# One store of a head's attention outputs in place of four, and a shorter probabilities' ring with the value products further behind, in a fused adaLN + cached attention + mixer MLP kernel

## The chip, the cores and the metric

The kernel runs on one core of one Trainium2 chip. A core has a matrix engine (TensorE, PE in the profile; its weight loads are shown as PEld), a vector engine (VectorE, DVE), a scalar engine (ScalarE, ACT), a general engine (GpSimd, POOL) and a sync engine (SP), which here only issues DMA transfers. Each takes its instructions in order, and they meet at semaphores. PSUM is the memory that matmuls write to, SBUF the working memory; DMA transfers run beside the engines.

The metric is the device time in microseconds (us) of one execution, as the median of several runs.

## The reference

One sequence of 2048 tokens of width 640, 32 attention heads of 128 with cached keys and values (2048 of each), and a mixer MLP; everything is bf16. Cut to what matters:

```python
mod = (silu(c) @ w_mod).reshape(1, 6, 1, -1)            # sa, ca, ga, sb, cb, gb
h = layernorm(x) * (1 + ca) + sa
q = (h @ wq), in heads                                  # 32 x 2048 x 128
p = softmax(q k^T * 128 ** -0.5)                        # per head 2048 x 2048
x = x + ga * ((p v), heads side by side) @ wo
h = layernorm(x) * (1 + cb) + sb
g = gelu(layernorm(h) @ w1); four column groups shifted by +1, -1, +2, -2 rows
x1 = h + shifted(g) @ w2
x = x + gb * (x1 + gelu(layernorm(x1) @ w3) @ w4)
```

## The kernel before, in words

Every operation is put in the program through a small helper, `Prog`, with the keys that it reads and writes; the helper works out the semaphore waits from them. The order on each engine is the order in which the program's loops write the operations down. There is no planner.

**Attention.** The work is cut in 512 tiles: 32 heads of 16 query tiles of 128 rows. A loop over steps s (line 506) writes down for each step what belongs to different tiles:

- the scores of tile s, in two halves of 1024 keys (`qk`, line 286, TensorE), into the PSUM tile `Sps`;
- the value product of tile s - `PVD`, `PVD` = 8 (`pv`, line 299, TensorE), also in two halves, in between the halves of the scores. Its weights are the transposed probabilities `PTs`; the values carry a column of ones, so that the row sums come with it;
- a part of the next head's query projection (`q_piece`, line 237);
- for every second finished product a copy from PSUM to `Of` (line 537, ScalarE);
- VectorE reduces each half of the scores to a minimum and writes the negated, scaled scores to `negS`, which has three slots (line 546). GpSimd takes the minimum of the two halves (line 556). ScalarE makes the exponential from `negS` with this bias (line 559), into `Pb`, a ring of `RP` = 10 slots, one tile each;
- the probabilities are transposed from `Pb` into `PTs`, a second ring of `RP` slots. Tiles 3 and 10 of a head are transposed on TensorE (`t_piece`, line 253) and evicted by ScalarE (line 262), one of the four halves by VectorE (line 264). The other fourteen go through DMA transposes that SP issues (`transpose`, line 222), two neighbours in one transfer where both are there: six pairs and two single tiles for a head;
- SP also issues the loads of the next heads' keys (line 205, step 2 of a head), query weights (line 209, step 6) and values (line 214, step `PVD` + 1 = 9). All of SP's transfers stand in one queue, in the order of the loop;
- `LAG` = 4 steps after its product GpSimd normalises a tile (`norm`, line 447) with the inverse row sums (`rcp`, line 440, for four tiles) into `On`, which has two buffers of four tiles. After each fourth tile GpSimd issues a store of 128 KB to `o_scratch` in DRAM (line 454), laid out [8, 128, 32, 2, 128]: pair of query tiles, row, head, tile of the pair, column. A piece that lies together there is 512 bytes, the two tiles of one row and head.

A product thus needs its probabilities transposed `PVD` steps after its scores; an exponential needs the slot of `Pb` of the tile `RP` before it read; a transpose needs the slot of `PTs` of the tile `RP` before it multiplied.

**After attention.** `load_ot` (line 495, SP) reads a pair of query tiles of all heads back from `o_scratch` with a transpose; then follow the output projection (line 618, TensorE), layer norms (lines 599 to 644) and the MLP (lines 706 to 769). These stages reuse SBUF: the rings hold `xt`, `xb` and one of the two buffers `gT` of the MLP's hidden activations, `On` holds statistics, `wo` holds `w3`, `w4` and the output's staging.

Of the kernel before, what the change touches and what calls it, by code (L numbers as in the profile page):

```python
# [7 lines left out]
BF16 = mybir.dt.bfloat16  # L8
# [107 lines left out]
def bass_adaLN_cond__mha_block_cached__mixer_s_mlp__prompt_kernel(  # L116
# [21 lines left out]
    with ExitStack() as es:  # L138
# [11 lines left out]
        if True:  # L150
            with ExitStack() as es1:
                sb1 = lambda name, shape, dt: es1.enter_context(nc.sbuf_tensor(name, shape, dt))
                RP = 10
                PVD = 8
# [3 lines left out]
                ring = sb1("ring", [128, 2 * RP, SK], BF16)  # L158
# [6 lines left out]
                On = sb1("On", [128, 2, 4, 128], BF16)  # L165
# [12 lines left out]
                Pb = ring[:, 0:RP]  # L178
                PTs = ring[:, RP:2 * RP].rearrange("p r (k q) -> p r k q", k=NKT)
# [5 lines left out]
                RO = 13 * SK  # L185
# [11 lines left out]
                assert CO + 8 * KT <= 2 * RP * SK and XO + NQT * D <= WO_ and WO_ + KT * 2 * D <= 10 * SK  # L197
# [19 lines left out]
                assert RP % 2 == 0 and NQT % 2 == 0  # L217
                is_pe = lambda g: g % NQT in PE_TILES

                def transpose(g, n):  # L220
                    b = g % RP
                    G.dma("sync", lambda e: e.dma_start_transpose(
                        PTs[:, b:b + n].rearrange("p r k q -> p (r k) q"), ring[:, b:b + n].rearrange("p r s -> p (r s)")),
                        ("t", b), r=[("Pb", b + i) for i in range(n)], w=[("PT", b + i, z) for i in range(n) for z in range(2)])
# [22 lines left out]
                def t_piece(g, r, q):  # L247
                    jb = bank(("t", g, r))

                    def f(t):  # L250
                        for z in range(4 * q, 4 * q + 4):
                            kt = 8 * r + z
                            ins = t.transpose(JBb[jb][:, z * 128:(z + 1) * 128], Pb[:, g % RP, kt * 128:(kt + 1) * 128], ident[:])
                        return ins
                    G.op("tensor", f, r=[("Pb", g % RP)], w=[("J", jb)])

                def t_evac(g, r):
                    jb = bank(("t", g, r))
                    dst = PTs[:, g % RP, r * 8:(r + 1) * 8, :]
                    src = JBb[jb].rearrange("p (k q) -> p k q", k=8)  # L260
                    if not by_dve(g, r):
                        G.op("scalar", lambda a: a.copy(dst, src), r=[("J", jb)], w=[("PT", g % RP, r)])  # L262
                    else:
                        G.op("vector", lambda v: v.tensor_copy(dst, src), r=[("J", jb)], w=[("PT", g % RP, r)])
# [27 lines left out]
                def pv(g, half):  # L292
                    hb = (g // NQT) % 2
                    b = g % RP
                    ob = PO[:, ((g // 2) % 2) * 512 + (g % 2) * 130:]

                    def f(t):
                        for kt in range(half * 8, half * 8 + 8):
                            ins = t.matmul(ob[:, 0:129], PTs[:, b, kt, :], Vaug[:, hb, kt, 0:129],  # L299
                                           start=(kt == 0), stop=(kt == NKT - 1))  # L300
# [3 lines left out]
                ringk = lambda a, b: [k for i in range(a // SK, -(-b // SK)) for k in (  # L304
                    [("Pb", i)] if i < RP else [("PT", i - RP, 0), ("PT", i - RP, 1)])]
                WMK = ringk(WO_, WO_ + KT * 2 * D)
                WRK = ringk(RO, 2 * RP * SK)
# [137 lines left out]
                def norm(gr, z):  # L445
                    b = gr % 2
                    G.op("gpsimd", lambda g: g.tensor_scalar(  # L447
                        out=On[:, b, z, :], in0=Of[:, 2 * b + z // 2, z % 2, 0:128],
                        scalar1=rl[:, 4 * b + z:4 * b + z + 1], scalar2=1.0, op0=ALU.mult, op1=ALU.mult),
                        r=[("Of", 2 * b + z // 2), ("rl", b)], w=[("On", b, z)])  # L450
                    if z < 3:
                        return
                    hh, jj = divmod(4 * gr, NQT)
                    G.dma("gpsimd", lambda e: e.dma_start(  # L454
                        o_scr[jj // 2:jj // 2 + 2, :, hh].rearrange("a p z d -> p a (z d)"),
                        On[:, b].rearrange("p (a z) d -> p a (z d)", a=2)),
                        ("o", b), r=[("On", b, z) for z in range(4)], w=[("os", b), ("osd", jj // 4, hh)])
# [5 lines left out]
                assert GT0 + NFT4 <= 2 * RP * SK  # L463
# [4 lines left out]
                gT = [flat[:, GT0:GT0 + NFT4].rearrange("p (f q) -> p f q", f=NFT),  # L468
                      negb[:, 0:NFT4].rearrange("p (f q) -> p f q", f=NFT)]
# [11 lines left out]
                sm = On[:].rearrange("p a z d -> p (a z d)").bitcast(F32)  # L481
# [4 lines left out]
                mhalf = sm[:, 384:385]  # L486
                NEG = [("negS", i) for i in range(3)]
# [3 lines left out]
                ONK = [("On", b, z) for b in range(2) for z in range(4)]  # L491
# [14 lines left out]
                for s in range(NG + PVD + LAG):  # L506
                    h, j = divmod(s, NQT)
                    g_ = s - PVD
# [26 lines left out]
                    if 0 <= g_ < NG and g_ % 2 == 1:  # L535
                        p = g_ // 2
# [18 lines left out]
                    if s < NG:  # L555
# [4 lines left out]
                            Pb[:, s % RP, :], negS[:, s % 3, :], ACT.Exp, bias=nm[:, r8:r8 + 1], scale=-1.0),  # L560
                            r=[("negS", s % 3), ("nm", r8)], w=[("Pb", s % RP)])
# [11 lines left out]
                    if 0 <= s - PVD - LAG:  # L573
                        gr, z = divmod(s - PVD - LAG, 4)
# [3 lines left out]
                    if s == NG:  # L578
# [3 lines left out]
                    if s == NG + 1:  # L582
# [154 lines left out]
                def d_op(cc, f_):  # L737
# [9 lines left out]
                    G.op("scalar", lambda a: a.activation(gT[g][0:fsz[f_], f_, :], JB[jb][0:fsz[f_], :], GELU),  # L747
                         r=[("J", jb)], w=[("gT", g)] + ([("OT", 1)] if g == 1 and f_ == 0 else []))

                def e_op(j):  # L750
# [5 lines left out]
                    def f(t):  # L756
                        for c0, cw in NC2:
                            for f_ in range(NFT):
                                ins = t.matmul(YB[b][:, c0:c0 + cw], gT[g][0:fsz[f_], f_, q0:q0 + 128], w4[0:fsz[f_], f_, c0:c0 + cw],  # L759
# [71 lines left out]
```

## Time and profile before

| what | value |
|---|---|
| median of three runs | 1615.55 us (1611.88 to 1622.05) |
| span of the profiled execution, first to last instruction | 1613.0 us, 34611 instructions |
| granted TensorE clock, mean | 0.993 |
| busy: PE, DVE, ACT, POOL | 92%, 86%, 80%, 39% of the span |
| DMA | 333.60 MB, mean 207 GB/s |
| last exponential of attention ends | about 1264 us |

No time of the profiled execution beyond its span is recorded; the median of the runs is 2.5 us above the span.

How to read the lines that follow: a group's row gives the line, the engine, the operation and the tiles written and read, then the number of instructions, their busy time and the mean of one in ns, and behind the last bar the idle time of the engine just before them with what ended it. A row of the waits gives the waiting engine and line, what ended the wait, the total in us, how often, and the longest. A row of the timeline gives the start in us, the duration, the engine (SPq is SP's queue) and the line; "x5" means that five neighbouring instructions are merged in the row; in square brackets stands the idle time before it. A queue's row gives its packets, megabytes and the time that its packets took, as a share of 16 engines' span.

### The profile page before, as it was taken

Reading aid. Unit: us, or ns where it says so; the run is one execution under the profiler, and the core shown is the slowest. Engines: PE = TensorE matmul, PEld = TensorE weight load, DVE = VectorE, ACT = ScalarE, POOL = GpSimd, SP = SyncE. Lnnn points to the kernel's source line nnn. Section 1 sums busy time; section 2 is a strip of 40 time slices with the busy share of each in tenths; the row PEclk is TensorE's granted clock in tenths of the full one; section 3 lists DMA queues with packets and bytes.
Section 4 is the critical chain, followed back from the end, with each engine's and each line's share of the span. In section 5 each row is a group of like instructions: output and inputs, shape, how many; then the busy total and the mean of one; then the engine's idle time right before and its main releaser. Section 6 shows DMA issues by size and latency. Waiting matters only on the chain.

```text
span 1613.0 us, 34611 instructions
## 1 busy us (share of the span) xinstructions
PE 1489.2 (92%) x13978; PEld 962.9 (60%) x14231; DVE 1394.3 (86%) x2460; ACT 1294.9 (80%) x1145; POOL 622.8 (39%) x1394
## 2 busy tenths in 40 slices
PE   5899999999999999999999999999999799999998
PEld 3466666666666666666666666666666555545444
DVE  6999999999999999999999999999999256665424
ACT  4999999999999999999999999999999300055330
POOL 0244444444444444444444444444444323222000
PEclk9999999999999999999999999999999799999999
DMA  9999999999999999999999999999999995530000
GB/s 305 231 230 234 243 238 235 241 242 242 233 243 236 244 232 242 238 235 238 242 249 229 245 237 233 245 237 233 241 237 245 214 213 105 105 111 1 17 17 34
DMA packets 1167728, 333.60 MB, mean 207 GB/s; under 512 B 1148304, under 2 KB 1161552, under 8 KB 1167568
## 3 DMA queue, kind: packets, MB, share of 16 engines
q1 hardware_dynamic: 1161424, 314.59, 97.5%
q0 software_dynamic: 6144, 16.79, 3.4%
q8 instruction: 112, 1.84, 0.5%
q14 instruction: 48, 0.39, 0.1%
HBM read 43.48 MB, written 19.40 MB: 39 GB/s over the span
## 4 chain that ended last, share of the span: by engine, by line
ACT 29%; DVE 24%; PE 21%; DMA 16%; issue 8%; POOL 2%; SPq 0%; POOLq 0%; DVEq 0%
ACT ring L559 23%; DVE negS L546 22%; DMA ring<-ring 13%; PE Sps L618 7%; PE Sps L759 4%; ACT ring L262 2%; PE Oaug L743 2%; PE QPp L743 2%; ACT Of L537 1%; ACT kv L244 1%; PE Sps L728 1%; PE PTp L299 1%; DMA ring<-in_A_x_dram 1%; POOL small L556 1%; PE Sps L286 1%
## 5 line engine op out<-in xcount | busy, mean ns | idle before, releaser
L546 DVE TENSOR_SCALAR_CACHE_REDUCE negS<-Sps 128x1024 f32<-128x1024 f32 x1024 | 1179.0, 1220 | 30.3 <-PE Sps L286 29.5
L559 ACT ACTIVATE ring<-negS,small 128x2048 bf16<-128x2048 f32 x512 | 1029.3, 2017 | 22.7 <-POOL small L556 20.5
L299 PEld LDWEIGHTS PTp<-kv,ring 128*128 128x128 bf16 x8192 | 553.0, 98 | 313.0 <-DMA ring<-ring 97.4
L299 PE MATMUL PTp<-kv,ring 128*128 128x129 bf16 x8192 | 647.9, 221 | 51.2 <-DMA ring<-ring 49.1
L286 PE MATMUL Sps<-kv 128*128 128x512 bf16 x1950 | 592.3, 381 | 35.6 <-DVE negS L546 18.1
L556 POOL TENSOR_SCALAR small<-small 128x1 f32<-128x1 f32 x512 | 145.9, 285 | 631.2 <-DVE negS L546 631.2
L286 PEld LDWEIGHTS Sps<-kv 128*128 128x128 bf16 x2048 | 144.7, 97 | 139.6 <-DVE negS L546 94.6
L447 POOL TENSOR_SCALAR On<-Of,small 128x128 bf16<-128x128 f32 x512 | 189.9, 371 | 13.4 <-DMA o_scratch<-On 0.5
L656 ACT COPY kv<-PTp 128x640 bf16<-128x640 bf16 x32 | 22.0, 692 | 154.8 <-PE PTp L653 154.8
L440 POOL TENSOR_TENSOR small<-Of,small 128x4 f32<-128x4 f32 x128 | 133.1, 1040 | 6.7 <-ACT Of L537 6.7
L454 POOL DMA_DIRECT2D o_scratch<-On x128 | 103.1, 806 | 40.8 <-POOL On L447 37.2
L537 ACT COPY Of<-PTp 128x259 f32<-128x259 f32 x256 | 95.7, 374 | 11.1 <-PE PTp L299 11.1
L237 PE MATMUL Oaug<-hTx,kv 128*128 128x512 bf16 x264 | 100.4, 385 | 3.9 <-DVE hTx L396 3.9
L237 PE MATMUL QPp<-hTx,kv 128*128 128x512 bf16 x259 | 97.7, 382 | 2.7 <-ACT hTx L391 2.2
L546 DVE DVE_READ_ACCUMULATOR negS<-Sps 128x1 f32 x1024 | 85.8, 84 | 0.0
L599 POOL TENSOR_SCALAR On<-On 128x1 f32<-128x1 f32 x48 | 24.3, 507 | 152.2 <-DVE On L608 152.2
L626 DVE TENSOR_TENSOR ring<-Sps,mod_bc 128x640 f32<-128x640 f32 x16 | 13.2, 824 | 77.6 <-PE Sps L618 77.6
L618 PE MATMUL Sps<-wo,hTx 128*128 128x128 bf16 (+1 forms) x504 | 71.2, 303 | 5.3 <-DMA hTx<-o_scratch 4.9
L618 PE MATMUL Sps<-wo,negS 128*128 128x128 bf16 (+1 forms) x504 | 69.1, 298 | 1.5 <-DMA negS<-o_scratch 1.1
L763 DVE TENSOR_TENSOR ring<-Sps,ring 128x640 f32<-128x640 f32 x16 | 13.2, 824 | 66.2 <-PE Sps L759 66.2
L262 ACT COPY ring<-Oaug 128x1024 bf16<-128x1024 bf16 x64 | 65.2, 1019 | 0.0
L618 PEld LDWEIGHTS Sps<-wo,hTx 128*128 128x128 bf16 x512 | 40.2, 99 | 36.6 <-DMA hTx<-o_scratch 4.8
(82 smaller groups left out, 1004.2 us busy)
## 6 DMA issues: line engine op xcount, KB each, us to landing
kv<-in_A_v_cache_dram SPq DMA_DIRECT2D x32, 512.0 KB, 5.0
o_scratch<-On POOLq DMA_DIRECT2D x128, 128.0 KB, 3.8
ring<-in_A_x_dram SPq DMA_DIRECT2D x8, 640.0 KB, 5.1
kv<-in_A_wq_dram SPq DMA_DIRECT2D x32, 160.0 KB, 3.4
wo<-in_A_wo_dram SPq DMA_DIRECT2D x1, 5120.0 KB, 16.5
ring<-ring SPq DMA_TRANSPOSE x256, 7.0
ring<-in_w_mod_dram SPq DMA_DIRECT2D x1, 3200.0 KB, 13.5
out_dram<-wo SPq DMA_DIRECT2D x16, 160.0 KB, 1.8
```

Of the source, the lines that this page charges most:

```text
L237: G.op("tensor", lambda t: t.matmul(JB[jb], wq[:, hb, q, :], hT[:, q, cc * 512:(cc + 1) * 512], start=(q == 0), stop=(q == KT - 1)), r=[(" ...
L262: G.op("scalar", lambda a: a.copy(dst, src), r=[("J", jb)], w=[("PT", g % RP, r)])
L286: ins = t.matmul(Sps[:, col:col + 512], QT[:, hb, j * 128:(j + 1) * 128], KTs[:, hb, col:col + 512], start=True, stop=True)
L299: ins = t.matmul(ob[:, 0:129], PTs[:, b, kt, :], Vaug[:, hb, kt, 0:129], start=(kt == 0), stop=(kt == NKT - 1))
L440: G.op("gpsimd", lambda g: g.tensor_tensor(out=rl[:, 4 * b:4 * b + 4], in0=Of[:].rearrange("p a z d -> p (a z) d")[:, 4 * b:4 * b + 4, 128 ...
L447: G.op("gpsimd", lambda g: g.tensor_scalar(out=On[:, b, z, :], in0=Of[:, 2 * b + z // 2, z % 2, 0:128], scalar1=rl[:, 4 * b + z:4 * b + z ...
L454: G.dma("gpsimd", lambda e: e.dma_start(o_scr[jj // 2:jj // 2 + 2, :, hh].rearrange("a p z d -> p a (z d)"), On[:, b].rearrange("p (a z) d ...
L537: G.op("scalar", lambda a, p=p: a.copy(Of[:, p % 4].rearrange("p z d -> p (z d)")[:, 0:259], PO[:, (p % 2) * 512:(p % 2) * 512 + 259]), r= ...
L546: G.op("vector", lambda v, half=half, s=s, r8=r8: v.tensor_scalar(out=negS[:, s % 3, half * 1024:(half + 1) * 1024], in0=Sps[:, half * 102 ...
L556: G.op("gpsimd", lambda g, r8=r8: g.tensor_scalar(out=nm[:, r8:r8 + 1], in0=nm0[:, r8:r8 + 1], scalar1=nm1[:, r8:r8 + 1], scalar2=None, op ...
L559: G.op("scalar", lambda a, s=s, r8=r8: a.activation(Pb[:, s % RP, :], negS[:, s % 3, :], ACT.Exp, bias=nm[:, r8:r8 + 1], scale=-1.0), r=[( ...
L618: ins = t.matmul(YB[b][:, c0:c0 + cw], OTj[pr % 2][:, 2 * hh + z, :], wo[:, hh, c0:c0 + cw], start=(hh == 0), stop=(hh == H - 1))
```

## The change

The ring of probabilities `Pb` gets 8 slots (`RPB`), the ring of transposed ones keeps 10 (`RPT`). The value products run 10 steps behind the scores (`PVD`); near the end of the last head the distance shrinks to 8 (`PVE`), by a table `PVS` of which products belong to which step, so that the last ones come in the same step as before. The values' load, at step `PVD` + 1 of a head, moves from step 9 to 11. `On` holds two whole heads, and a head's sixteen normalised tiles are stored by one transfer of 512 KB after its last tile; the last head still stores four tiles at a time. Tiles that shared the freed memory move: `wmodr` in the set-up, and in the MLP the first buffer `gT`, which is now in three pieces (in the ring, in `On`, and in the rest of `wo`).

```diff
-                RP = 10
-                PVD = 8
+                RPB, RPT = 8, 10
+                PVD, PVE = 10, 8
...
-                ring = sb1("ring", [128, 2 * RP, SK], BF16)
+                ring = sb1("ring", [128, RPB + RPT, SK], BF16)
...
-                On = sb1("On", [128, 2, 4, 128], BF16)
+                On = sb1("On", [128, 2, NQT, 128], BF16)
...
-                RO = 13 * SK
+                RO = 10 * SK
...
                 def transpose(g, n):
-                    b = g % RP
+                    b, t = g % RPB, g % RPT
                     G.dma("sync", lambda e: e.dma_start_transpose(
-                        PTs[:, b:b + n].rearrange("p r k q -> p (r k) q"), ring[:, b:b + n].rearrange("p r s -> p (r s)")),
-                        ("t", b), r=[("Pb", b + i) for i in range(n)], w=[("PT", b + i, z) for i in range(n) for z in range(2)])
+                        PTs[:, t:t + n].rearrange("p r k q -> p (r k) q"), ring[:, b:b + n].rearrange("p r s -> p (r s)")),
+                        ("t", b), r=[("Pb", b + i) for i in range(n)], w=[("PT", t + i, z) for i in range(n) for z in range(2)])
...
                 def norm(gr, z):
                     b = gr % 2
+                    hh, jj = divmod(4 * gr + z, NQT)
                     G.op("gpsimd", lambda g: g.tensor_scalar(
-                        out=On[:, b, z, :], in0=Of[:, 2 * b + z // 2, z % 2, 0:128],
+                        out=On[:, hh % 2, jj, :], in0=Of[:, 2 * b + z // 2, z % 2, 0:128],
                         scalar1=rl[:, 4 * b + z:4 * b + z + 1], scalar2=1.0, op0=ALU.mult, op1=ALU.mult),
-                        r=[("Of", 2 * b + z // 2), ("rl", b)], w=[("On", b, z)])
-                    if z < 3:
+                        r=[("Of", 2 * b + z // 2), ("rl", b)], w=[("On", hh % 2, jj)])
+                    n = 4 if hh == H - 1 else NQT
+                    if jj % n < n - 1:
                         return
-                    hh, jj = divmod(4 * gr, NQT)
+                    j0 = jj + 1 - n
                     G.dma("gpsimd", lambda e: e.dma_start(
-                        o_scr[jj // 2:jj // 2 + 2, :, hh].rearrange("a p z d -> p a (z d)"),
-                        On[:, b].rearrange("p (a z) d -> p a (z d)", a=2)),
-                        ("o", b), r=[("On", b, z) for z in range(4)], w=[("os", b), ("osd", jj // 4, hh)])
+                        o_scr[j0 // 2:(j0 + n) // 2, :, hh].rearrange("a p z d -> p a (z d)"),
+                        On[:, hh % 2, j0:j0 + n, :].rearrange("p (a z) d -> p a (z d)", z=2)),
+                        ("o", hh % 2, j0 if n < NQT else 0), r=[("On", hh % 2, j0 + i) for i in range(n)],
+                        w=[("osd", i, hh) for i in range(j0 // 4, (j0 + n) // 4)])
...
+                def gT(g, f_):
+                    if g == 1:
+                        return negb[:, f_ * 512:f_ * 512 + 512]
+                    if f_ < g0:
+                        return flat[:, GT0 + f_ * 512:GT0 + f_ * 512 + 512]
+                    if f_ < g0 + g1:
+                        return Onf[:, 1024 + (f_ - g0) * 512:1024 + (f_ - g0) * 512 + 512]
+                    return gx[:, (f_ - g0 - g1) * 512:(f_ - g0 - g1) * 512 + 512]
...
                 LAG = 4
-                for s in range(NG + PVD + LAG):
+                PVS, at = {}, []
+                for g in range(NG):
+                    d = max(PVE, min(PVD, PVE + (NG - 12 - g) // 2))
+                    at.append(max(g + d, at[-1] if g else 0))
+                    PVS.setdefault(at[g], []).append(g)
+                assert all(len(v) <= 2 for v in PVS.values())
+                NORMS = {}
+                for g in range(NG):
+                    NORMS.setdefault(at[g] + LAG, []).append(g)
+                OT0 = max(NG, at[NG - NQT + 3] + LAG + 1)
+                for s in range(at[-1] + LAG + 1):
                     h, j = divmod(s, NQT)
-                    g_ = s - PVD
+                    pvs = PVS.get(s, [])
...
-                        if 0 <= g_ < NG:
-                            pv(g_, half)
+                        for g_ in pvs:
+                            if len(pvs) == 1:
+                                pv(g_, half)
+                            elif g_ == pvs[half]:
+                                pv(g_, 0)
+                                pv(g_, 1)
...
                         G.op("scalar", lambda a, s=s, r8=r8: a.activation(
-                            Pb[:, s % RP, :], negS[:, s % 3, :], ACT.Exp, bias=nm[:, r8:r8 + 1], scale=-1.0),
-                            r=[("negS", s % 3), ("nm", r8)], w=[("Pb", s % RP)])
+                            Pb[:, s % RPB, :], negS[:, s % 3, :], ACT.Exp, bias=nm[:, r8:r8 + 1], scale=-1.0),
+                            r=[("negS", s % 3), ("nm", r8)], w=[("Pb", s % RPB)])
...
-                    if 0 <= s - PVD - LAG:
-                        gr, z = divmod(s - PVD - LAG, 4)
+                    for g_ in NORMS.get(s, []):
+                        gr, z = divmod(g_, 4)
                         if z == 0:
                             rcp(gr)
                         norm(gr, z)
-                    if s == NG:
+                    if s == OT0:
                         load_ot(0)
```

For the 512 tiles of this case `OT0` is step 512, as before.

More of the change, by code (lines that the diff above doesn't have):

```diff
@@ L177, in bass_adaLN_cond__mha_block_cached__mixer_s_mlp__prompt_kernel @@
                 QT = kv[:, o3:o3 + 2 * SQ].rearrange("p (b q) -> p b q", b=2)
-                Pb = ring[:, 0:RP]
-                PTs = ring[:, RP:2 * RP].rearrange("p r (k q) -> p r k q", k=NKT)
+                Pb = ring[:, 0:RPB]
+                PTs = ring[:, RPB:RPB + RPT].rearrange("p r (k q) -> p r k q", k=NKT)
                 flat = ring[:].rearrange("p r s -> p (r s)")
@@ L293, in pv @@
                     hb = (g // NQT) % 2
-                    b = g % RP
+                    b = g % RPT
                     ob = PO[:, ((g // 2) % 2) * 512 + (g % 2) * 130:]
@@ L490, in bass_adaLN_cond__mha_block_cached__mixer_s_mlp__prompt_kernel @@
                 HTK = [("hT", cc, k) for cc in range(NQC) for k in range(KT)]
-                ONK = [("On", b, z) for b in range(2) for z in range(4)]
+                ONK = [("On", b, z) for b in range(2) for z in range(NQT)]
                 OFK = [("Of", b) for b in range(4)]
@@ L534, in bass_adaLN_cond__mha_block_cached__mixer_s_mlp__prompt_kernel @@
                                     evacs.append((t_evac, g, r))
-                    if 0 <= g_ < NG and g_ % 2 == 1:
-                        p = g_ // 2
+                    for p in [g_ // 2 for g_ in pvs if g_ % 2 == 1]:
                         G.op("scalar", lambda a, p=p: a.copy(
```

35 lines of the change are left out of this document (19 added, 16 removed).

## The prediction

> **What bounds the kernel now.** I began with the groups by cost and the queues of the page, went on to the list of waits, and then to the timeline of SP's queue, which decides.
>
> ```profile
> q1 hardware_dynamic: 1161424, 314.59, 97.5%
> q0 software_dynamic: 6144, 16.79, 3.4%
> ...
> L546 DVE TENSOR_SCALAR_CACHE_REDUCE negS<-Sps 128x1024 f32<-128x1024 f32 x1024 | 1179.0, 1220 | 30.3 <-PE Sps L286 29.5
> ...
> PEld PTp L299 <- DMA ring<-ring: 97.4, 105, 3.1
> ```
>
> The attention stage runs to about 1264 us, and in it VectorE is nearly full. Two of its 1024-wide reductions start 1.144 us apart in the timeline, so a head needs 16 x 2.288 + 0.60 (its one eviction of line 264) = 37.2 us. It idles 30.3 us in all, for late scores; by heads, 6.0 of that lies in the first. TensorE stands in order behind value products (line 299) that wait for DMA transposes, and its scores come late for that. So at most 24 us can be won from such waits. ScalarE is no refuge: by the distance of starts (1.90 us an exponential, 0.25 an `Of` copy, 0.46 a `QT` copy, 0.89 an eviction of line 262) a head costs it 30.4 + 2.0 + 1.8 + 2.7 = 36.9 us.
>
> The question is whether those transposes are late through too short a lead or because their queue is full. SP's timeline (start, duration, issuing line):
>
> ```profile
> 76.11 3.98 SPq L222 DMA_TRANSPOSE ring<-ring  x1
> ...
> 597.54 0.58 SPq L209 DMA_DIRECT2D kv<-in_A_wq_dram  x1
> 598.17 9.10 SPq L222 DMA_TRANSPOSE ring<-ring  x2
> 607.31 0.58 SPq L214 DMA_DIRECT2D kv<-in_A_v_cache_dram  x1
> 607.94 20.87 SPq L222 DMA_TRANSPOSE ring<-ring  x5
> 628.85 2.00 SPq L205 DMA_TRANSPOSE kv<-in_A_k_cache_dram  x1
> ```
>
> Each row begins 0.04 to 0.05 us after the one before has ended: SP issues without a break, and a pair's issue takes 4.2 to 5.5 us where an undisturbed pair took 3.98 (first row). Is SP waiting inside those durations? Take the pair of tiles 236 and 237 (line 222 has eight rows to a head; counted from the start, this is the seventh of head 14):
>
> ```profile
> 606.39 2.02 ACT L559 ACTIVATE ring<-negS,small 128x2048 bf16<-128x2048 f32 x1
> ...
> 611.91 5.49 SPq L222 DMA_TRANSPOSE ring<-ring  x1
> ...
> 619.62 0.47 PEld L299 LDWEIGHTS PTp<-kv,ring 128*128 128x128 bf16 x8 [0.66 <-DMA ring<-ring]
> ```
>
> Its probabilities were done at 608.41, SP reached it only at 611.91, it landed at 619.58 and its product started at 619.62. In the first head, where nothing queues, the issue starts 0.02 us after the exponential ends, so waits lie before a row, not in it. (The list of SP's waits names ACT for 613 us; that is ScalarE's counter moving while an issue runs.) From head 3 to head 28 the first transpose of a head comes every 38.27 us, of which 37.76 are issues and 0.5 the eleven small gaps. SP with the DMA engines behind it is the bound, at 38.3 us a head against 37.2 of VectorE.
>
> **The change part by part.** Durations are of the profiled execution, whose span is 1613.0 us; the three runs shown have a median of 1615.55, 2.5 above it, so I add 2.5 at the end.
>
> *Products ten tiles behind (line 299).* They come two steps later, 2 x 2.29 = 4.6 us. Before, the pair's probabilities ended 11.2 us before its landing (619.58 - 608.41) when the product was found waiting; that room becomes 15.8. It removes no issue from SP, so in the steady stage SP's backlog merely grows from about 4 us to 8 and every landing is again waited for.
>
> *Probabilities' ring of 8.* New wait: line 559 of tile g+8 needs tile g transposed. Exponential g+8 starts 7 x 2.29 - 2.0 = 14.0 us after exponential g+1 ends. Behind it on ScalarE stand `Of` and `QT` copies, and VectorE feels it once `negS`, three deep, is full: an exponential ends 5.2 us after its first reduction starts (3.2 in the median plus 2.0), the third next reduction starts after 6.87, so 1.67 us more are covered. 14.0 + 1.67 = 15.7: the two new limits meet. The gain in room is 15.7 - 11.3 = 4.4 us, once, not per head.
>
> What is it worth? In the last head no K and V load is left, and SP runs dry:
>
> ```profile
> 1259.08 3.98 SPq L222 DMA_TRANSPOSE ring<-ring  x1
> ...
> 1264.05 4.60 SPq L222 DMA_TRANSPOSE ring<-ring  x1
> 1268.69 9.71 SPq L495 DMA_TRANSPOSE hTx<-o_scratch  x1
> ```
>
> It waits 1.96 us before 1259.08 and 0.99 before 1264.05. Work that arrives 4.4 us sooner fills these 3.0 us and no more: **-3 us**.
>
> *V load at step 11 in place of 9.* Same load, one issue later; buffers are free (the last product of the old head is in step 9). SP needs 0.58 us for it either way, and the excess of the next issue (4.06 us median for the single tile behind it, against 1.96 for the other single) moves to the next pair: 0.
>
> *Stores.* 128 issues of 0.81 us on POOL become 31 of 512 KB and 4 of 128 KB. POOL is idle 61% of the span; its total is worth nothing. On the DMA engines q0 takes 3.4% of 1613 us, 54.8 us, or 1.71 a head. The bytes and the 512-byte rows stay; 93 completions go. Issues that had a store's packets inside were not longer than those without (pairs from tiles 8 and 12 of a head, with one: 4.54 and 4.63 us in the mean; from 6 and 14, without: 4.51 and 4.40), so a store costs SP 0 to 0.2 us, and its merging between -0.6 and +0.7 us a head (the upper end below). I take 0, nearest to these rows; both ends go into the range.
>
> The length of one long issue is not in the trace. Below: 0.81. Above: fourfold rows, 3.2. SP's direct loads take 0.58 us at 160 KB as at 512, which speaks for the lower end; I take 1.4 us, which is just hidden: line 556's wait behind a store shows 0.56 us of spare (0.81 + 0.56 = 1.37).
>
> *Tail.* From tile 497 the lag shrinks to 8 and the last tile's product stays in its old step; so do the last head's four stores. The first read of `o_scratch` starts at 1268.69 as SP comes free, and its store was issued at 1261.43 and landed 5.9 later, 1267.3. Now head 30's 512 KB go two steps ahead on the same queue: **+1 us** (0 to 2). The set-up and the placing of `gT` in three pieces change addresses only: 0.
>
> **Sum:** 1613.0 - 3 + 1 = 1611 in the profile, 1611 + 2.5 = 1613 us.
>
> A page speaks against the store. The Trainium skill, "DMA: Bandwidth & Descriptors", section "Latency and other measured facts", reports 207 GB/s for copies with a row pitch of 512 KiB and 164 at 2 MiB. The new transfer steps through eight rows 2 MiB apart for each partition where the old one stepped through two, and if that held, 1.71 us a head would become, as an estimate from that page, 2.16, or +14 us in all. No run here shows it yet.
>
> **The rivals.**
>
> *Relief (faster).* The four bursts do hold up the transposes and one does not; the excess of 4.4 us over 3.98 partly goes. For it: a pair is slower than undisturbed. Against: the issues without a store. SP then falls to VectorE's 37.2 us, and 24 us of idle go: 1613.0 - 24 + 2.5 = 1592.
>
> *A long issue on POOL (slower).* In the step of a head's store, line 556 of the next tile stands behind it, and ScalarE's exponential waits for that.
>
> ```profile
> 1233.36 0.81 POOL L454 DMA_DIRECT2D o_scratch<-On  x1 [0.29 <-POOL On L447]
> 1234.75 0.28 POOL L556 TENSOR_SCALAR small<-small 128x1 f32<-128x1 f32 x1 [0.58 <-DVE negS L546]
> ```
>
> At 3.2 us it comes 3.2 - 1.37 = 1.8 us late; ScalarE, with at most 0.7 us in hand there, loses about 1.1 and has 36.9 + 1.1 + 0.7 (its present waits for POOL, 20.5 us over 32 heads) = 38.7 a head, 0.4 over SP: 31 x 0.4 = +13 us. From 2.8 us on it decides, and each further us costs 31; at 3.5 us, 31 x 0.7 = 22: 1613 + 22 = 1635.
>
> *A dearer store (slower).* The page's rule above as a mechanism of this kernel: the store's packets take longer and SP's engines with them. Stores land in 2.7 us at best and 3.8 in the median; by that ratio, 1.41, a head pays 0.70 more, 31 x 0.70 = +22: 1635. Against it: stores left no mark on the issues.
>
> *Only an exchange.* The ring of 8 takes back what the later products give, ScalarE waits where TensorE did: 1613.0 + 1 + 2.5 = 1616.
>
> **How the numbers follow.** One per cent, 16 us, is about what a measurement tells from no change here (the three runs spread over 10). Forecast 0.40 (1613); exchange 0.14; relief 0.24 (1592); long issue 0.13; dearer store 0.09, all of it over 1%. Same: 0.40 + 0.14 = 0.54; faster 0.24; slower 0.22. The likeliest cases alone span 1608 to 1620. The range reaches to relief's floor and to both slower rivals: 1592 to 1636, leaving out the ends of each.
>
> **What would show it.** Right: SP's rows still touch from head 1 to 30, at 38.3 us a head; the chain of probabilities' end to landing grows from 11 to about 15 us; line 299's waits for DMA stay or pass to line 559 and line 546; VectorE still idles some 24 us. Relief: SP's issues near 4.0 us, breaks between them, VectorE's idle time near 6. Long issue: line 454 above 2.8 us and line 559 waiting for line 556. Dearer store: q0's share above 3.4% and SP's issues longer in the step of a store. What would make me wrong is that the transposes' rate depends on how they queue, which no row of before can show.

## The result, and the profile after

The changed kernel takes 1639.64 us (median of four runs, 1632.02 to 1645.65) against 1615.24 us before: a ratio of 1.0148, 95% interval 1.012 to 1.0176. It is slower, and lies outside the range of 1592 to 1636 us.

The page of the profile after, its queues and two of its groups (the reductions are line 574 now, the exponentials line 587):

```profile
span 1643.9 us, 34707 instructions
...
q1 hardware_dynamic: 1161424, 314.59, 97.2%
q0 software_dynamic: 4656, 16.78, 3.6%
...
L574 DVE TENSOR_SCALAR_CACHE_REDUCE negS<-Sps 128x1024 f32<-128x1024 f32 x1024 | 1178.9, 1220 | 60.2 <-PE Sps L286 56.2
L587 ACT ACTIVATE ring<-negS,small 128x2048 bf16<-128x2048 f32 x512 | 1033.0, 2027 | 58.9 <-DMA ring<-ring 47.5
```

The span grew by 30.9 us, and VectorE's idle time ahead of its reductions by 29.9, from 30.3 to 60.2. Its last reduction ends at 1289.9 us in place of 1260.4; what comes behind it takes 354.0 us in place of 352.6. So the loss lies in the attention stage, and in waits. (This execution took 1645.65 us, the longest of the four; by the medians the loss is 24.4 us.) The list of waits of after (waiting line, what ended it; total, times, longest):

```profile
PEld PTp L299 <- DMA ring<-ring: 75.3, 52, 7.1
...
PE PTp L299 <- DMA ring<-ring: 53.3, 31, 6.7
ACT ring L587 <- DMA ring<-ring: 47.5, 31, 6.5
```

There are fewer waits for transposes than the 105 before, but single ones last up to 7.1 us, where 3.1 was the longest; and ScalarE now waits for them too. The transposes by their line (duration of an issue in ns: least, median, most) and the stores (count, size, median us from issue to landing), first before and then after:

```profile
L222 SPq DMA_TRANSPOSE ring<-ring x256: 1662/4337/6717, 45.1 to 1264.0; - x128
...
o_scratch<-On POOLq DMA_DIRECT2D x128, 128.0 KB, 3.8
```

```profile
L222 SPq DMA_TRANSPOSE ring<-ring x256: 1600/4344/11041, 44.7 to 1295.7; - x128
...
o_scratch<-On POOLq DMA_DIRECT2D x31, 512.0 KB, 7.2
```

The median has not moved; the longest issue has gone from 6.7 to 11.0 us, and a store lands in 7.2 us in place of 3.8. The longest issue, in the timeline of after (start, duration, line), SP first, then POOL, ScalarE and VectorE:

```profile
567.93 0.58 SPq L209 DMA_DIRECT2D kv<-in_A_wq_dram  x1
568.56 18.26 SPq L222 DMA_TRANSPOSE ring<-ring  x3
...
573.29 11.04 SPq L222 DMA_TRANSPOSE ring<-ring  x1
...
573.20 0.98 POOL L456 DMA_DIRECT2D o_scratch<-On  x1 [0.30 <-POOL On L448]
...
587.26 2.00 ACT L587 ACTIVATE ring<-negS,small 128x2048 bf16<-128x2048 f32 x1 [6.07 <-DMA ring<-ring]
...
589.59 1.22 DVE L574 TENSOR_SCALAR_CACHE_REDUCE negS<-Sps 128x1024 f32<-128x1024 f32 x1 [6.56 <-PE Sps L286]
```

The row of 18.26 us merges three issues; the second of them is the row of 11.04. POOL issues a head's store at 573.20, SP begins a pair's transpose at 573.29, and neither gets on. The store lands at 584.46. The transpose's issue ends at 584.33 and it lands at 587.18; the exponential that needs its ring slot starts at 587.26, after a wait of 6.07 us, and VectorE loses 6.56 us. What the DMA engines moved meanwhile, by stretches of the same trace (the last column is GB/s):

```profile
core 0: us, PE busy (x) PEld busy (x) DVE busy (x) ACT busy (x) POOL busy (x), PEclk, DMA share, GB/s
564.00:573.00 9.00, 8.85 (x97) 6.15 (x97) 9.00 (x17) 9.00 (x9) 3.53 (x9) 1.00 1.19 229
575.50:583.50 8.00, 5.29 (x47) 3.07 (x46) 7.07 (x14) 5.69 (x5) 2.63 (x8) 1.00 1.21 119
...
1096.00:1104.00 8.00, 6.83 (x66) 4.15 (x65) 7.97 (x15) 7.22 (x6) 3.55 (x9) 1.00 1.22 232
```

The engines count as just as busy (1.21), but move 119 GB/s in place of 229. The last row is another head's store, issued at 1094.94, 0.70 us behind the start of a pair's issue: there the rate stays at 232 GB/s, and the transposes took 4.36 and 4.35 us. By the timeline, in six of the 31 heads a pair's issue began within 0.25 us of the store's; those six issues took 9.05 us in the mean (5.8 to 11.0), the nearest pairs of the other 25 stores 4.99. Six times 4.06 us is 24 us of issue time, but that is not the loss itself: the run with products eight behind, below, loses more with two such issues. What counts in these six is the order: the four that began up to 0.1 us behind the store took 9.2 to 11.0 us, the two that began up to 0.1 us ahead of it 5.8 and 7.7.

### The profile page after: what moved, and what is told of

Its sections match the earlier page's. It is cut to its first block, busy times and chain, and to the rows that moved or that the text cites. A ratio compares the mean times of both kernels' runs of the same rounds, so it can differ in the third digit from the quotient of the medians.

```text
span 1643.9 us, 34707 instructions
## 1 busy us (share of the span) xinstructions
PE 1502.5 (91%) x13978; PEld 968.5 (59%) x14231; DVE 1394.3 (85%) x2460; ACT 1289.9 (78%) x1145; POOL 551.4 (34%) x1301
## 3 DMA queue, kind: packets, MB, share of 16 engines
q0 software_dynamic: 4656, 16.78, 3.6%
## 4 chain that ended last, share of the span: by engine, by line
DVE 24%; ACT 24%; DMA 21%; PE 21%; issue 9%; SPq 1%; POOL 0%; ACTq 0%
DVE negS L574 22%; DMA ring<-ring 20%; ACT ring L587 18%; PE Sps L646 7%; PE Sps L787 4%; PE Oaug L771 2%; PE QPp L771 2%; ACT Of L565 2%; ACT kv L244 2%; ACT ring L262 1%; PE Sps L756 1%; PE Sps L286 1%; PE PTp L299 1%; DMA ring<-in_A_x_dram 1%; DMA negS<-o_scratch 1%
## 5 line engine op out<-in xcount | busy, mean ns | idle before, releaser
L574 DVE TENSOR_SCALAR_CACHE_REDUCE negS<-Sps 128x1024 f32<-128x1024 f32 x1024 | 1178.9, 1220 | 60.2 <-PE Sps L286 56.2
L587 ACT ACTIVATE ring<-negS,small 128x2048 bf16<-128x2048 f32 x512 | 1033.0, 2027 | 58.9 <-DMA ring<-ring 47.5
L299 PEld LDWEIGHTS PTp<-kv,ring 128*128 128x128 bf16 x8192 | 562.0, 99 | 305.5 <-DMA ring<-ring 75.3
L286 PE MATMUL Sps<-kv 128*128 128x512 bf16 x1949 | 599.4, 385 | 48.1 <-DVE negS L574 28.8
L286 PEld LDWEIGHTS Sps<-kv 128*128 128x128 bf16 x2048 | 133.9, 98 | 166.1 <-DVE negS L574 124.7
L646 PEld LDWEIGHTS Sps<-wo,negS 128*128 128x128 bf16 x512 | 39.5, 98 | 32.1 <-DMA negS<-o_scratch 1.8
```

What stands on the lines that cost most here:

```text
L286: ins = t.matmul(Sps[:, col:col + 512], QT[:, hb, j * 128:(j + 1) * 128], KTs[:, hb, col:col + 512], start=True, stop=True)
L574: G.op("vector", lambda v, half=half, s=s, r8=r8: v.tensor_scalar(out=negS[:, s % 3, half * 1024:(half + 1) * 1024], in0=Sps[:, half * 102 ...
L587: G.op("scalar", lambda a, s=s, r8=r8: a.activation(Pb[:, s % RPB, :], negS[:, s % 3, :], ACT.Exp, bias=nm[:, r8:r8 + 1], scale=-1.0), r=[ ...
L646: ins = t.matmul(YB[b][:, c0:c0 + cw], OTj[pr % 2][:, 2 * hh + z, :], wo[:, hh, c0:c0 + cw], start=(hh == 0), stop=(hh == H - 1))
```

## The experiments

All ratios are against the kernel before on the same chip. Theory A, formed from the rows above, was that a large store from POOL and a transpose from SP in flight together hold each other up. Its rivals were the short ring (B), the store's rows 2 MiB apart (C), the moved load of the values (D), and that any store costs its bytes (E).

### Four stores again, in the changed kernel

```diff
-                    n = 4 if hh == H - 1 else NQT
+                    n = 4
```

> The changed kernel with four stores of 128 KB a head again (the last head's form for all heads); rings of 8 and 10 and products ten tiles behind stay. Theory A (the one big store gets between the packets of a DMA transpose and stalls both, 10 to 11 us for an issue that else takes 4.3): the long issues go, none over 7 us, and the time falls to 0.99 to 1.00 of before, 1600 to 1616 us. Theory B (the ring of 8 makes ScalarE wait for transposes, whatever the store): 1.01 to 1.02 of before as with the change, ScalarE's exponential still waits some 45 us for DMA.

Measured: 1.0074 (1.0055 to 1.0094), 1627.84 us. Half the loss goes with the one store. The longest issue is 7.8 us; five are over 7, all of them the pair behind the values' load. Neither theory had 0.7%: something besides the store costs, and the moved load was still in this kernel.

### The one store, products eight behind

```diff
-                PVD, PVE = 10, 8
+                PVD, PVE = 8, 8
```

> The changed kernel with the products eight tiles behind as before (and so the values' load at step 9); ring of 8 and the one store stay. Theory A: still slower than before, 1.01 to 1.03, with issues of 9 us and more; ScalarE's waits for DMA go, TensorE's take their place. Theory B: the ring no longer decides, since TensorE waits first: 1.00 of before.

Measured: 1.0206 (1.0183 to 1.0229). Theory B falls: TensorE waits first again, and it is slower than the change, not equal to before. The rows of this run, the transposes and VectorE's waits:

```profile
L574 DVE TENSOR_SCALAR_CACHE_REDUCE negS<-Sps 128x1024 f32<-128x1024 f32 x1024 | 1178.3, 1220 | 62.6 <-PE Sps L286 62.2
...
L222 SPq DMA_TRANSPOSE ring<-ring x256: 1636/4328/10008, 45.4 to 1295.6; - x128
```

Only two issues are over 7 us here; yet VectorE idles 62.6 us. The issues nearest to a store that do not start with it are longer too, 5.20 us in the mean. The rare long issue is the extreme of a broader cost, which the next run locates.

### The ring of 8 alone

Both edits above together:

```diff
-                PVD, PVE = 10, 8
+                PVD, PVE = 8, 8
...
-                    n = 4 if hh == H - 1 else NQT
+                    n = 4
```

> Four stores and products eight behind, so that only the ring of 8 slots (and the placing of buffers) is left of the change. Theory A: 1.00 of before, SP busy without a break at 38.2 us a head. Theory B: 1.01 or more.

Measured: 1.0014 (1.0001 to 1.0026). As A had it: the ring costs 0.1%, and SP's issues with their small gaps fill 38.36 us of a head's 38.40.

This run and the one before it differ in the stores alone. By their timelines (means of heads 2 to 30), one store in place of four lengthens the pair from tile 8, beside which it now falls, from 4.58 to 5.61 us and the single tile 11 behind it from 4.08 to 5.07; a head's other six transposes together shorten from 25.67 to 24.51.

### No stores in the changed kernel

```diff
                     j0 = jj + 1 - n
+                    if hh < H - 1:
+                        return
...
-                    G.dma("sync", lambda e: e.dma_start_transpose(OTj[pr % 2], o_scr[pr].rearrange("q h z d -> q (h z d)")),
+                    G.dma("sync", lambda e: e.dma_start_transpose(
+                        OTj[pr % 2], A_v_cache[0].rearrange("(a b) (c e) d -> a (b c) (e d)", a=8, c=32)[pr]),
```

> The changed kernel without the stores of the first 31 heads: left out of the computation, the output projection reads the same number of bytes from the value cache in place of o_scratch. Theory A (the store and a transpose in flight together stall each other): SP idles between issues, VectorE sets the pace at 37.2 us a head, no issue over 7 us: 0.975 to 0.985 of before, 1575 to 1592 us. If instead the later products or the values' load cost by themselves, it stays at 0.99 to 1.00 with SP busy throughout.

Measured: 0.979 (0.9775 to 0.9805), 1584.04 us, as A had it: with no stores the rings, the later products and the moved load cost nothing that shows, and VectorE sets the pace at 37.28 us a head. One sign of A failed: five issues are still over 7 us, up to 7.7, all behind the values' load, so such an issue alone does not tell of a store. VectorE's row:

```profile
L577 DVE TENSOR_SCALAR_CACHE_REDUCE negS<-Sps 128x1024 f32<-128x1024 f32 x1024 | 1174.7, 1222 | 6.3 <-PE Sps L286 6.0
```

### The one store issued by SP

```diff
-                    G.dma("gpsimd", lambda e: e.dma_start(
+                    G.dma("sync", lambda e: e.dma_start(
                         o_scr[j0 // 2:(j0 + n) // 2, :, hh]...
```

> The changed kernel with the same one store of a head issued by SP, in its queue behind the transposes, in place of POOL; bytes and rows are the same. Theory A, in the form that the packets of two queues interleave: within one queue the store runs by itself for some 1.4 us, no issue over 7 us, 0.98 to 0.995 of before. Theory C (the store is dear in itself, by its 512-byte rows 2 MiB apart): still 1.01 or more. Theory E (any store costs SP its bytes): 1.00.

Measured: 0.9993 (0.9977 to 1.0009). The same 512 KB in the same rows, in one queue with the transposes, cost 1.5% less than from POOL. Its issues of the store and of transposes:

```profile
L222 SPq DMA_TRANSPOSE ring<-ring x256: 1393/4400/7370, 45.2 to 1263.9; - x128
...
o_scratch<-On SPq DMA_DIRECT2D x31, 512.0 KB, 4.0
```

The store lands in 4.0 us (7.2 from POOL in the changed kernel). A's meeting of two queues is gone, but the time is E's 1.00 and not A's 0.98 to 0.995: without stores it was 0.979, so a store costs in this queue too. The three issues over 7 us that remain are those behind the values' load.

### Padded rows in DRAM

```diff
-        o_scr = nc.dram_tensor("o_scratch", [NQT // 2, 128, H, 2, DH], BF16)
+        o_scr = nc.dram_tensor("o_scratch", [NQT // 2, 129, H, 2, DH], BF16)
...
```

The store and the later read take rows 0 to 127.

> The changed kernel with o_scratch padded, so that the eight rows that a partition stores lie 2 MiB + 16 KiB apart in place of 2 MiB. Theory C: the store lands faster and the long issues go: 0.99 to 1.005 of before. Theory A: no change, 1.01 to 1.02.

Measured: 1.0135 (1.0069 to 1.02), with issues up to 8.9 us. The interval holds the change's own 1.0148, and the stores land in 6.7 us in the median against 7.2. Theory C's 0.99 to 1.005 is excluded and nothing here supports it; as this run's times spread over more than 20 us, a part below 1% is not excluded.

### The values' load at step 11, in the kernel before

```diff
-                        if j == PVD + 1 and h + 1 < H:
+                        if j == 11 and h + 1 < H:
                             load_v(h + 1)
```

> The kernel before with only the values' load moved from step 9 to step 11 of a head. Theory D (part of the later products' cost in the run with four stores, +0.7%, is this load, whose 512 KB now lie under the pair behind it): 1.005 to 1.01 of before. Otherwise, the deeper queue or the ring is what costs there, and this is 1.00 (0.997 to 1.003).

Measured: 1.0068 (1.0045 to 1.0091). This one line explains what the run with four stores had left. In the means of heads 2 to 30 the single tile 11 is issued in 2.38 us in place of 4.14, but the pair behind the load takes 6.61 in place of 4.68, and those from tiles 6 and 14 another 0.1 and 0.25.

### The values' load back in its place, in the changed kernel

```diff
-                        if j == PVD + 1 and h + 1 < H:
+                        if j == 10 and h + 1 < H:
                             load_v(h + 1)
```

> The changed kernel with the values' load at step 10 of a head: no transpose is issued in step 10, so in SP's queue the load stands where it stood in the kernel before, behind the pair 8 and 9 and ahead of tile 11. If the load's place and the store add up: 1.0148 - 0.0068 = 1.008 of before (1.005 to 1.011), 1624 to 1633 us. If the products ten behind are worthless beside the store, as the run with products eight behind suggests: 1.02.

Measured: 1.0215 (1.0197 to 1.0234): the two do not add up. The expected sum, 1.008, was wrong. Beside one store, the load at its old place makes the kernel slower than at the new one, the other way round than beside four. This run and the one with products eight behind have the same SP queue and differ in `PVD` alone: 1.0215 and 1.0206. Ten behind is worth nothing that shows; the 3 us (0.2%) that the prediction gave it are within these intervals.

### Both: store from SP, load back

```diff
-                        if j == PVD + 1 and h + 1 < H:
+                        if j == 10 and h + 1 < H:
...
-                    G.dma("gpsimd", lambda e: e.dma_start(
+                    G.dma("sync", lambda e: e.dma_start(
                         o_scr[j0 // 2:(j0 + n) // 2, :, hh]...
```

> The changed kernel with the one store issued by SP and the values' load at step 10. By sum of the two effects, 0.9993 - 0.0068 = 0.9925 of before (0.989 to 0.997), some 1604 us: faster than both kernels. If the load's place matters only beside stores of POOL: 1.00 as without it.

Measured: 1.0069 (1.0053 to 1.0085). Slower than with the load at step 11 (0.9993), so that sum fails too. For both places of the load, SP's queue is 1.5% better for the store than POOL's; for both queues, a single store goes 0.7% better with the load at 11. Neither of the two expectations, 0.9925 and 1.00, was met.

### Rows of 4 KB

```diff
-        o_scr = nc.dram_tensor("o_scratch", [NQT // 2, 128, H, 2, DH], BF16)
+        o_scr = nc.dram_tensor("o_scratch", [H, 128, NQT, DH], BF16)
...
-                        o_scr[j0 // 2:(j0 + n) // 2, :, hh].rearrange("a p z d -> p a (z d)"),
+                        o_scr[hh, :, j0:j0 + n].rearrange("p z d -> p (z d)"),
...
```

> The changed kernel with the head's store written as 128 rows of 4 KB that lie together, in place of 1024 rows of 512 bytes; the same bytes, queue and moment. (The later reads take the same bytes in an order that does not fit, so the outputs after attention are not the reference's; no time depends on that.) If what interleaves badly is a matter of the packets of 4 KB, which stay: 1.01 to 1.02 as with the change. If the many short rows make the store long and so the collision: 0.995 to 1.005.

Measured: 1.005 (1.0032 to 1.0067). With an eighth of the rows two thirds of the loss go, though the packets stay at 4 KB and their number at 4656 on POOL's queue. The rows of POOL's issue and of the transposes:

```profile
L222 SPq DMA_TRANSPOSE ring<-ring x256: 1594/4360/8044, 45.0 to 1275.9; - x128
...
o_scratch<-On POOLq DMA_DIRECT2D x31, 512.0 KB, 6.1
```

POOL's issue itself shortens from 0.98 to 0.64 us. Six pairs began together with a store here too; they took 5.7 us, not 9.05.

### No stores in the kernel before

```diff
                     hh, jj = divmod(4 * gr, NQT)
+                    if hh < H - 1:
+                        return
```

The output projection reads from the value cache here too.

> The kernel before without the stores of its first 31 heads, else as the run without stores of the changed kernel: it prices the four small stores. If four small stores cost what one on SP's queue costs (1.4 us of SP a head) the period falls to VectorE's 37.2 to 37.5 us: 0.978 to 0.987 of before. If they cost nothing, as the prediction took: 1.00.

Measured: 0.9812 (0.9798 to 0.9827). Four stores of 128 KB cost 1.9%, not nothing. SP's timeline in this run, and VectorE's reductions (line 549 here):

```profile
594.94 0.58 SPq L214 DMA_DIRECT2D kv<-in_A_v_cache_dram  x1
595.56 20.28 SPq L222 DMA_TRANSPOSE ring<-ring  x5
615.88 2.08 SPq L205 DMA_TRANSPOSE kv<-in_A_k_cache_dram  x1
618.01 4.39 SPq L222 DMA_TRANSPOSE ring<-ring  x1
...
L549 DVE TENSOR_SCALAR_CACHE_REDUCE negS<-Sps 128x1024 f32<-128x1024 f32 x1024 | 1174.5, 1219 | 6.6 <-PE Sps L286 6.6
```

SP's rows touch here as well (issues and small gaps fill 37.20 us of a head's 37.27), although VectorE idles only 6.6 us in all and sets the pace. Where the 1.0 us a head had been can be read from the issues (means of heads 2 to 30, with the stores and without):

| pair or tile | 0, 1 | 2 | 4, 5 | 6, 7 | 8, 9 | 11 | 12, 13 | 14, 15 |
|---|---|---|---|---|---|---|---|---|
| store in flight during the issue, us | 3.1 | 0.2 | 3.5 | 1.2 | 2.9 | 0.7 | 2.9 | 0.6 |
| issue with stores, us | 4.73 | 2.15 | 5.00 | 4.49 | 4.57 | 4.14 | 4.68 | 4.40 |
| issue without, us | 4.48 | 2.11 | 4.64 | 4.62 | 4.38 | 4.29 | 4.50 | 4.27 |

The four pairs that run beside a store for some 3 us are 0.25, 0.36, 0.19 and 0.18 us longer with it, 0.98 in all; the other four together are 0.11 shorter.

### Two stores, and eight

Two: the run with the ring of 8 alone, with eight tiles in a store for all heads but the last. Eight: the kernel before, with a store after each second tile. In both, the later read waits by pair of tiles.

```diff
-                    n = 4 if hh == H - 1 else NQT
+                    n = 4 if hh == H - 1 else 8
```

```diff
-                    if z < 3:
+                    if z % 2 == 0:
                         return
-                    hh, jj = divmod(4 * gr, NQT)
+                    hh, jj = divmod(4 * gr + z - 1, NQT)
...
-                        o_scr[jj // 2:jj // 2 + 2, :, hh].rearrange("a p z d -> p a (z d)"),
-                        On[:, b].rearrange("p (a z) d -> p a (z d)", a=2)),
+                        o_scr[jj // 2, :, hh].rearrange("p z d -> p (z d)"),
+                        On[:, b, z - 1:z + 1].rearrange("p z d -> p (z d)")),
...
```

> The run with ring of 8 and products eight behind, with two stores of 256 KB a head (four of 128 KB in the last head); four gave 1.0014 of before and one 1.0206. Theory A with a cost that grows with the size of a store: between them, 1.005 to 1.015, longest issues between 7 and 9 us. If the count of stores costs: below 1.0014 or at it.

> The kernel before with eight stores of 64 KB a head in place of four of 128 KB, each after a pair of tiles; nothing else changed. Theory A with a cost that grows faster than the size: SP's issues shorten and the time falls to 0.988 to 0.998 of before, faster than both kernels. If each store costs by itself (its issue on POOL of 0.8 us, its completion): 1.005 to 1.02. If only the bytes cost: 1.00.

Measured: two 1.013 (1.0106 to 1.0153), eight 0.9991 (0.9976 to 1.0006). With products eight behind and the load in SP's old place, the count of stores a head gives this row (the ring has 10 slots in the first three columns, 8 in the last two; the period is the mean distance of the first transposes of heads 1 to 31):

| stores a head | none | 8 x 64 KB | 4 x 128 KB | 2 x 256 KB | 1 x 512 KB |
|---|---|---|---|---|---|
| ratio to before | 0.981 | 0.999 | 1.000 (1.001 with the ring of 8) | 1.013 | 1.021 |
| head's period, us | 37.27 | 38.14 | 38.26 (38.40) | 39.03 | 39.33 |

The price rises with the size of one store above 128 KB, and below it hardly falls: eight gained nothing beyond the interval, as if the bytes alone cost there. (With their number the stores' places among the transposes change too; the two are not separated here.) The run with two stores lies where A had it, but without the long issues of 7 to 9 us that A expected:

```profile
L222 SPq DMA_TRANSPOSE ring<-ring x256: 1711/4363/6895, 44.5 to 1287.5; - x128
```

So 1.3% is lost without one issue over 7 us.

### The values' load at step 15, in the changed kernel

```diff
-                        if j == PVD + 1 and h + 1 < H:
+                        if j == 15 and h + 1 < H:
                             load_v(h + 1)
```

> The changed kernel with the values' load at step 15 of a head, well behind the head's store of step 13. If it is the store beside the values' load that stalls: no issue over 7 us at the pair from tile 8, 0.995 to 1.005 of before. If the store beside a transpose alone does it: 1.01 to 1.02, with such issues left.

Measured: 1.0211 (1.0185 to 1.0238). It is not the load beside the store that stalls: well apart, the kernel is slower than with the load at step 11. The pair from tile 8, which meets the store, has two issues over 7 us and takes 5.55 us in the mean, as in the run with the load back (5.55).

## Why the prediction was wrong

**What bounds the kernel.** Right in the main: SP's queue and the DMA engines behind it set the pace at 38.3 us a head against VectorE's 37.2, and taking DMA work away let VectorE set it. But one reading in it was weaker than it looked. That SP's rows touch does not show a bound: in the kernel before without stores they touch too, at VectorE's pace. What showed it was that products started as their transposes landed, and, in the experiments, that the time fell when DMA work went.

**Products ten behind, ring of 8.** Small, as forecast; the size was not resolved. The waits of SP in the last head that the -3 us were to fill, 1.96 and 0.99 us, are gone in the trace of after (0.04 each). But 8 and 10 behind gave 1.0206 and 1.0215 at the same order of SP's queue, each to about 0.2%, which neither shows 3 us nor excludes them. The ring gave 1.0014. The two limits did meet, ScalarE waiting for 47.5 us where it had not waited before.

**The values' load.** Costed at 0, it was worth +0.7% beside four stores (1.0068) and -0.7% beside one. The step had the excess of the issue behind the load move to the next pair, and it did: 1.76 us went from tile 11 and 1.93 came to the pair behind. But the head's period grew by 0.4 us, part of it at the pairs from tiles 6 and 14, and the step counted that issue alone. Why other issues change, and why the sign turns beside one store, is not shown.

**The stores.** This is the step that failed most: "a store costs SP 0 to 0.2 us, and its merging between -0.6 and +0.7 us a head", taken at 0. Four cost 38.26 - 37.27 = 1.0 us a head, 0.25 for each, little above that range; one of 512 KB costs 39.33 - 37.27 = 2.1, where the sum had put no more than four. So the merging costs 1.1 us a head and not 0, beyond the upper end of 0.7; over 30 heads that is 32 us, and by the medians of the runs with four and with one store, products eight behind, 31 (1.0014 and 1.0206). The change's own 24 us are 0.6 to 0.7% less, with its load at step 11; that figure is taken from the change's own time and is no second check.

The comparison that the step rested on was of unlike issues. It set the pairs from tiles 8 and 12 against those from 6 and 14 and left out the pairs from tiles 0 and 4, which run beside a store as long. Set against the same tiles without stores, the four pairs beside a store were 0.98 us a head longer (the table above). And what it had found for stores of 128 KB it took for one of 512 KB, on the ground that the bytes and rows stay. The price of a store is not settled by its bytes: in SP's queue the same store costs 1.5% less, and in pieces of 128 KB 1.9% less. (All prices are lower bounds, since without stores VectorE's pace hides what SP would have to spare.) The prediction's last sentence named the risk, that the transposes' rate depends on how they queue, but gave it no size.

**POOL's long issue.** 0.98 us measured, inside its bounds of 0.81 and 3.2 and below the 1.4 taken. ScalarE waits 10.6 us for line 584 in all, against 20.5 before. This rival fell. (Two of the prediction's small sums are off by rounding: 31 x 0.4 is 12 and not 13 us, and the gain in room, 15.7 less the 11.2 worked out above it, is 4.5 and not 4.4; neither changes the forecast.)

**The tail.** +1 us forecast, 1.4 measured (354.0 against 352.6).

**The rivals.** Relief came only without stores. The dearer store gave nearly the time, 1635 us, and both of its signs came: q0's share is 3.6% in place of 3.4, and the issues at the store are longer. But it had the store dear by rows 2 MiB apart, and padding them left the time within the interval (the stores landed in 6.7 us in place of 7.2), while the same rows from SP's queue cost 1.5% less; that the time came near is luck. The rule that it drew from the Trainium skill, "DMA: Bandwidth & Descriptors", section "Latency and other measured facts", was also a poor fit: that row is about the distance of rows from one partition to the next, here 16 KiB, and the four stores had the same 2 MiB between a partition's rows as the one, so the estimate of +14 us had no ground. No run here tests the page's own case. Two other sentences of that page bear on what did happen. Its "Rules for kernel authors" advise to coalesce many small transfers into one large one (below 64 KB most is overhead, it says); here one of 512 KB for four of 128 KB, which are above that size, cost 1.9% (1.0206 over 1.0014). And its section "Issuing engines are not separate DMA queues" says that issuing from several engines "will only save the time on the sequencer"; moving one store from POOL to SP took 1.5% off. For this kernel the measurements decide.

**What stays open.** Why two queues hold each other up is not shown. The traces show that the rate halves while the engines count as busy, that 4 KB rows and a common queue help, and that a transpose begun within 0.2 us behind the store's issue is worst. How a DMA engine shares its time between the two queues, and why the load's place has opposite signs beside one and four stores, no run here shows. No version here beats the kernel before beyond its interval; eight stores come nearest, at 0.9991.

## What to carry to other kernels

Where the DMA queue is the bound, price a transfer by a run without it, not by the issues that it happens to overlap. A large background store from one queue beside latency-bound transposes from another can cost more than the same bytes in pieces or in the transposes' own queue; before merging, try what the larger transfer does to whatever waits for the queue. To see what a transfer costs its neighbours, compare the same issue with and without it, not one issue with another. Deeper buffering does not empty a full queue: here it was worth nothing that showed, and it moved a load that was not free.

## What the runs showed of the hardware that was not expected

- A store of 512 KB in 512-byte rows from POOL and a pair's DMA transpose that SP begins within 0.2 us behind it hold each other up. In four traces (the change, products eight behind, the load back, the load at step 15) there are eleven such pairs: their issues took 8.3 to 11.0 us, and the stores landed in 8.9 to 11.3 us, where 7 is the median. Pairs begun up to 0.25 us ahead of the store took 5.0 to 7.7. In the one stretch looked at, the core moved 119 GB/s in place of 229.
- The same store in SP's queue lands in 4.0 us and costs 1.5% less time.
- POOL's issue of a store grows little with its size: 0.61 us for 64 KB, 0.81 for 128 KB, 0.98 for 512 KB in 512-byte rows, 0.64 for 512 KB in 4 KB rows (medians).
